# Recurrent memory attention on one core: row statistics, scaling and turning moved within a segment, and the copies of attention sums given to ScalarE

## The chip, the cores and the metric

The kernel runs on one core of a Trainium2 chip. The metric is the device time of one execution in microseconds (us); lower is better. TensorE (PE) multiplies matrices, VectorE (DVE) and ScalarE (ACT) do elementwise work, GpSimd (POOL) and SyncE (SP) mostly issue DMAs here. PEld is the loading of matmul weights. Each engine works through its own list of instructions in order and waits on semaphores for the others.

## The reference

```python
xn = layernorm(x)                                   # x: 2048 x 1024, bf16
# A: 64 segments of 32 rows, one after the other
for s in range(64):
    h = concat(mem, xn[32*s:32*s+32])               # 8 memory rows + 32 rows
    q, k, v = h @ Wq, h @ Wk, h @ Wv                # 32 heads of 128
    p = softmax(mask(q @ k.T * 128**-0.5))
    o = (p @ v) @ Wo                                # back to 1024 columns
    mem = o[:8]                                     # memory of the next segment
    out_A[s] = o[8:]
# B: a gated MLP on the 2 rows of xn with the largest xn @ w_r, added to those rows
return x + out_A + (xn + scatter(MLP(top 2 rows)))
```

Every segment needs the memory rows of the one before, so the 64 segments are a chain. Each uses all of Wq, Wk, Wv and Wo (32 MB in bf16).

## The kernel before

**Weights.** Wq, Wk, Wv and Wo are cut into 64 granules of 512 KB. 44 stay in SBUF. The other 20 are streamed again for every segment: SyncE issues their DMAs (line 368, `g<-wsc` in the trace) into five slots, and a slot is filled again when the last matmul that reads it is done. Two of the 20 are held in part or whole in PSUM and copied back (`BK<-KEPT`, `g<-KEPT`).

**Main rows and left rows.** A segment's matmuls take 32 rows: 24 main rows of the segment (`XM`) and the 8 memory rows. The 8 left rows of each segment (`XL`) do not depend on the memory for q, k and v, so those of four segments are gathered: a group G is four segments with j = 0, 1, 2, 3, and the 32 left rows of group G+1 are multiplied in passing while group G's weights are there (`PSl<-...`, `left_pass`). They are loaded in the segment with j = 0 (`get_left`, tile `BX`, a POOL DMA), normalised, turned, and are ready as `STL` at the end of that segment. Segments with j = 1, 2, 3 have no such work. Of the 16 segments with j = 0, those of groups 1 to 14 (s = 4 to 56) do it in the steady form.

**A segment in the program.** Six phases p = 0 to 5 (q and k of the first 16 heads, q and k of the second, v of both) with eight granules kc = 0 to 7 each (line 854). Then the output projection, w = 0 to 15, two heads each (`project`, lines 576 and 580). Other work is hung between matmuls by a table: `hook(p, kc, fn)` runs fn when the program reaches that place, and so fixes the order on every engine. Hooks of one place run in the order in which they were set.

- `scores(half)` multiplies q and k of 16 heads and does the mask, the maximum and its subtraction on DVE (lines 674 to 689). `exponent` is one ACT instruction (693). `soften` does sum, reciprocal, scaling and transposes on DVE (698 to 722). `attend(half, ph)` multiplies with v (739, 741) and copies the sums to SBUF (750 to `OT`, 752 to `OTL`).
- The layer norm of the next 24 rows has its steps apart. `part_stats` (198, 199) and `split_stats` (202 to 205) are DVE work on a quarter row per partition, `sum_stats` two small matmuls (209), `take_sums` an ACT copy (213), `spread_of` two DVE instructions (216, 218), `root_of` two ACT instructions (221, 222). `norm_seg` then scales on DVE (293 to 298: `XN`, and x itself in place, as the residual), `norm_left` does so for the left rows (341).
- `turn_rows` transposes `XN`, and in j = 0 the left rows, on PE (305) into the PSUM bank `BT`; `new_st` copies them on ACT to `ST` (319) and `STL` (323). In that bank also lie the second half of each block of attention sums (`OPB`) and the statistics' sums (`SUMS`).
- After w = 15, DVE adds up the result (928), PE turns it and DVE puts the memory rows into `ST` (328): the next segment's matmuls begin.

Of the kernel before, what the change touches and what calls it, by code (L numbers as in the profile page):

```python
# [51 lines left out]
def kernel(  # L52
# [16 lines left out]
    nc = tc.nc  # L69
# [8 lines left out]
    NSEG = S // SEG  # L78
    NT = S // P
# [74 lines left out]
    X = [const.tile([P, 256], BF16, name=f"X{b}") for b in range(2)]  # L154
# [13 lines left out]
    ROWS = [SW[:, 10:14], SW[:, 16:20]]  # L168
# [28 lines left out]
    def part_stats(x):  # L197
        nc.vector.bn_stats(out=S6, in_=x)
        nc.vector.bn_aggr(out=AV, in_=S6)
# [7 lines left out]
    def sum_stats(sums):  # L207
        for c in range(2):
            nc.tensor.matmul(sums, lhsT=S4, rhs=HL[:, 2 * c:2 * c + 2], start=(c == 0), stop=(c == 1),
                             skip_group_check=True)  # L210

    def take_sums(r, sums):
        nc.scalar.copy(out=r[:, 0:2], in_=sums)  # L213

    def spread_of(r):
        nc.vector.scalar_tensor_tensor(out=r[:, 2:3], in0=r[:, 0:1], scalar=r[:, 0:1], in1=r[:, 1:2],
                                       op0=ALU.mult, op1=ALU.subtract)
        nc.vector.tensor_scalar(out=r[:, 2:3], in0=r[:, 2:3], scalar1=0.0, scalar2=1e-5, op0=ALU.min, op1=ALU.subtract)

    def root_of(r):  # L220
        nc.scalar.activation(out=r[:, 3:4], in_=r[:, 2:3], func=ACTF.Ln, scale=-1.0)
        nc.scalar.activation(out=r[:, 3:4], in_=r[:, 3:4], func=ACTF.Exp, scale=-0.5)
# [66 lines left out]
    def norm_seg(s):  # L289

        x = X[s % 2]
        ab, m, r = AB, ROWS[0][:, 0:1], ROWS[0][:, 3:4]
        nc.vector.tensor_scalar(out=ab[:, 0:1], in0=r, scalar1=1.0, scalar2=KMSK, op0=ALU.add, op1=ALU.mult)
        nc.vector.tensor_scalar(out=ab[:, 1:2], in0=m, scalar1=r, scalar2=NMSK, op0=ALU.mult, op1=ALU.mult)
        xn = front.tile([P, 256], BF16, tag="st", name="XN")
        nc.vector.tensor_scalar(out=xn[:, :], in0=x[:, :], scalar1=m, scalar2=r,
                                op0=ALU.subtract, op1=ALU.mult)
        nc.vector.tensor_scalar(out=x[:, :], in0=x[:, :], scalar1=ab[:, 0:1], scalar2=ab[:, 1:2],
                                op0=ALU.mult, op1=ALU.add)
        return xn  # L300

    def turn(src, at=0):
        PTx = PTB[:, 256 * at:256 * (at + 1)].rearrange("p (c g r) -> p c g r", c=2, g=4)
        for c in range(2):
            nc.tensor.transpose(out=PTx[:, c, :, :].rearrange("p g r -> p (g r)"), in_=src[:, c * P:(c + 1) * P],
                                identity=IDENT[:, :])
        return PTx

    def gview(st):
        return st.rearrange("p (g c) r -> p c g r", c=2)  # L310

    def turn_rows(xn, xl):

        return turn(xn), turn(xl, 1) if xl is not None else None

    def new_st(turned):
        PTx, PTl = turned
        st = front.tile([P, KC, SEG], BF16, tag="st", name="ST")
        nc.scalar.copy(out=gview(st)[:, :, :, 0:XM], in_=PTx[:, :, :, 0:XM])
        if PTl is None:  # L320
            return st, None
        stl = one.tile([P, KC, SEG], BF16, tag="stl", name="STL")
        nc.scalar.copy(out=gview(stl), in_=PTl[:, :, :, :])
        return st, stl
# [15 lines left out]
    def norm_left(t):  # L340
        nc.vector.tensor_scalar(out=t[:, :], in0=t[:, :], scalar1=ROWS[1][:, 0:1], scalar2=ROWS[1][:, 3:4],
                                op0=ALU.subtract, op1=ALU.mult)
# [112 lines left out]
    xn = norm_seg(0)  # L455
# [178 lines left out]
    for s in range(NSEG):  # L634
        G, j = divmod(s, 4)
# [6 lines left out]
        QT, KT, PTs, OT, nxt, sums = {}, {}, {}, {}, {}, {}  # L642
        hooks = {}

        def hook(p, kc, fn):
            hooks.setdefault((p, kc), []).append(fn)
# [79 lines left out]
        def attend(half, ph, turn_too=None):  # L726
            if half not in sums:
                if half not in OT:
                    OT[half] = one.tile([P, 4, 4, SEG], BF16, tag=("kt", "bC")[half], name="OT")
                if half == 0:  # L730
                    nxt["wo"] = psA.tile([P, 512], F32, tag="acc", name="WO")
                sums[half] = [BS[:, 0:4 * NK] if half else nxt["wo"][:, 256:256 + 4 * NK], OPB]
            PTm, PTl = PTs[half]
            with_sums = (half, ph) == (0, 1) and s + 1 < NSEG
            for il in range(4):
                for jl in range(2):
                    q0 = 32 * (2 * ph + jl)
                    o = sums[half][jl][:, il * NK:(il + 1) * NK]
                    nc.tensor.matmul(o, lhsT=VM[half][q0:q0 + 32, il * P:(il + 1) * P], rhs=PTm[q0:q0 + 32, il, 0:NK],  # L739
                                     start=True, stop=False, tile_position=(q0, 0), skip_group_check=True)  # L740
                    nc.tensor.matmul(o, lhsT=VL[half][q0:q0 + 32, il * P:(il + 1) * P], rhs=PTl[q0:q0 + 32, il, 0:NK],
                                     start=False, stop=True, tile_position=(q0, 0), skip_group_check=True)
            if with_sums:
                sum_stats(SUMS)
            if turn_too is not None:
                turn_too()
            for jl in range(2):
                ov = sums[half][jl].rearrange("p (i q) -> p i q", i=4)
                copy = nc.scalar.copy if half == 0 or jl == 0 or ph == 1 else nc.vector.tensor_copy
                copy(out=OT[half][:, 2 * ph + jl, :, :], in_=ov[:, :, 0:SEG])  # L750
                h0 = 16 * half + 8 * ph + 4 * jl
                copy(out=left_out()[:, h0:h0 + 4, j, :], in_=ov[:, :, SEG:NK])
            if with_sums:
                take_sums(ROWS[0], SUMS)
# [57 lines left out]
        if j == 0 and G + 1 < NT:  # L812
            hook(*((4, 1) if s == 0 else (1, 0)), get_left)
            if s > 0:
                hook(2, 5, lambda: part_stats(nxt["xl"]))
                hook(2, 5, split_stats)
                hook(4, 0, lambda: sum_stats(SUMS))
                hook(4, 1, lambda: take_sums(ROWS[1], SUMS))
                hook(4, 2, lambda: spread_of(ROWS[1]))
                hook(5, 0, lambda: root_of(ROWS[1]))  # L820
            else:
                hook(5, 7, lambda: stats_now(nxt["xl"], ROWS[1]))
        hook(*((1, 0) if s > 0 else (2, 3)), clear_pl)
# [2 lines left out]
        hook(3, 4, lambda: soften(0))  # L826
        if s + 1 < NSEG:
            hook(2, 4, lambda: load_seg(s + 1))
        if j == 0 and G + 1 < NT:
            hook(5, 3 if s > 0 else 7, lambda: norm_left(nxt["xl"]))  # L830
        if s + 1 < NSEG:
            hook(4, 5, lambda: part_stats(X[(s + 1) % 2][:, :]))
        hook(4, 6, lambda: scores(1))
        hook(5, 0, exponent)
        if s + 1 < NSEG:
            hook(5, 0, split_stats)
        else:
            hook(1, 0, router_out)
            hook(1, 6, router_in)
# [49 lines left out]
        assert not hooks, hooks  # L889

        WO = nxt["wo"]
        if s + 1 < NSEG:
            root_of(ROWS[0])
            xn = norm_seg(s + 1)
            left_too = nxt["xl"] if j == 0 and G + 1 < NT else None
            turned = []

        def lhs_main(h):
            return OT[h // 16][:, (h % 16) // 4, h % 4, :]
# [2 lines left out]
        for w in range(16):  # L902
            if w == 5:
                attend(1, 0)
            if w == 8 and s + 1 < NSEG:
                attend(1, 1, lambda: turned.append(turn_rows(xn, left_too)))
                nxt["st"], stl = new_st(turned[0])
                STL = stl or STL
            elif w == 8:
                attend(1, 1)  # L910
            Gv = granule(48 + w)
            if w == N_WIDE:
                SUM = one.tile([P, 256], F32, tag="bE", name="SUM")
                add_halves(WO, X[s % 2], SUM, SUM)
                WO = psA.tile([P, 512], F32, tag="acc", name="WO")
            project(WO, w, Gv, lhs_main)
            held[48 + w] = Gv
            run_passes(6, w)
            if w == 9 and s + 1 < NSEG:
                new_lx(s + 1)  # L920
                bring_back(2, nc.scalar.copy)
            if w == 12 and s + 1 < NSEG:
                bring_back(0, nc.scalar.copy)
            if w == 2 and j == 3:
                xl_of[0] = load_left(G, one.tile([P, 256], BF16, tag="stl", name="OL")[:, :], True)
            release(6, w)
# [133 lines left out]
```

## Time and profile before

| | |
|---|---|
| median of 3 runs | 1890.1 us (1883.99 to 1893.26) |
| profiled execution | 1895.79 us, span 1894.1 us |
| mean granted TensorE clock | 0.949 |
| busy: PE, DVE, ACT, POOL | 85%, 53%, 41%, 24% of the span |
| DMA | 707.70 MB, mean 374 GB/s |

The first segment fills SBUF and copies the streamed weights; it ends at about 120 us. The last ends about 58 us before the end, where the MLP of the two rows follows. Between them lie 63 segments of some 27 us each. A row of the trace is read so: start, duration, engine, line, operation, what it writes and reads, how many, and in brackets the idle time of the engine just before and who ended it. Segments are told apart by the addition on line 928, which ends each.

### The profile page before, as it was taken

The numbers are of one execution on the slowest core, as the hardware profiler recorded it, in microseconds if no ns is written. First come the engines' busy times: TensorE is split into PE (matmuls) and PEld (weight loads), VectorE is DVE, ScalarE is ACT, GpSimd is POOL, SyncE is SP. The second block draws the span as 40 slices with busy tenths as digits, with TensorE's granted clock in tenths as the row PEclk, the third lists the DMA queues.
The fourth block names the chain that finished last, engine by engine and source line by source line (L and its number), as shares of the span: only waits on it lengthen the run. The fifth ranks groups of instructions, "written<-read, shape, count | busy, mean of one in ns | idle before, by whom it ended". The sixth has DMA issues, their size and how long they took to land.

```text
span 1894.1 us, 78902 instructions
## 1 busy us (share of the span) xinstructions
PE 1605.4 (85%) x33752; PEld 828.0 (44%) x33752; DVE 1010.8 (53%) x3368; ACT 768.8 (41%) x2409; POOL 455.2 (24%) x895
## 2 busy tenths in 40 slices
PE   4478989998988898899899888889889888989864
PEld 2134444444444444444444444444444444444433
DVE  2135566556555555655565555556555565565550
ACT  1034444444443444444444344444444444444330
POOL 2212313231231323123131322323132222312220
PEclk9579999999999999999999999999999999999995
DMA  9999999999999999999999999999999999999998
GB/s 368 404 366 377 365 374 381 370 385 366 380 362 376 342 373 383 372 383 355 387 370 378 363 378 377 359 381 376 388 362 376 379 377 382 365 384 373 366 402 341
DMA packets 228063, 707.70 MB, mean 374 GB/s; under 512 B 38912, under 2 KB 52832, under 8 KB 227712
## 3 DMA queue, kind: packets, MB, share of 16 engines
q1 hardware_dynamic: 190272, 666.72, 92.6%
q0 software_dynamic: 28640, 28.03, 4.6%
q10 hardware_dynamic: 8800, 7.92, 1.2%
q8 instruction: 264, 4.33, 0.9%
q14 instruction: 87, 0.71, 0.1%
HBM read 689.86 MB, written 22.29 MB: 376 GB/s over the span
## 4 chain that ended last, share of the span: by engine, by line
DMA 59%; PE 30%; DVE 6%; ACT 2%; issue 2%; POOL 1%; SPq 0%; DVEq 0%; ACTq 0%; POOLq 0%
DMA g<-wsc 46%; PE PSm L854 16%; PE PSl L567 4%; DMA BX<-in_A_x_dram 3%; PE WO L580 2%; PE BT L651 2%; DMA wres<-in_A_Wk_dram 1%; PE WO L576 1%; DMA g<-in_A_Wo_dram 1%; DMA g<-in_A_Wv_dram 1%; DMA wres<-in_A_Wv_dram 1%; DMA MW<-in_B_w_gate_dram 1%; PE WL L600 1%; DMA MW<-in_B_w_up_dram 1%; DMA X<-in_A_x_dram 1%
## 5 line engine op out<-in xcount | busy, mean ns | idle before, releaser
L854 PE MATMUL PSm<-wres,ST 128*32 128x512 bf16 x8448 | 702.5, 383 | 25.0 <-DMA wres<-in_A_Wv_dram 14.3
L854 PEld LDWEIGHTS <-ST 128*32 128x32 bf16 x12288 | 324.8, 96 | 392.3 <-issue 167.9
L854 PE MATMUL PSm<-g,ST 128*32 128x512 bf16 x3588 | 363.7, 388 | 84.2 <-DMA g<-wsc 70.0
L873 ACT CAST XB<-PSm 128x512 bf16<-128x512 f32 x256 | 150.3, 587 | 281.6 <-PE PSm L854 270.9
L483 POOL DMA_DIRECT2D LX<-ql_d x63 | 35.5, 564 | 655.5 <-PE WO L580 377.1
L567 PE MATMUL PSl<-wres,STL 128*32 128x512 bf16 x2112 | 184.5, 390 | 0.2 <-ACT XBl L878 0.2
L666 DVE COPY KT<-BT 128x512 bf16<-128x512 bf16 x112 | 45.8, 409 | 255.1 <-PE BT L651 252.4
L930 POOL DMA_DIRECT2D out_dram<-X x256 | 129.4, 512 | 210.7 <-DVE X L928 204.8
L286 POOL DMA_DIRECT2D X<-in_A_x_dram x252 | 127.4, 511 | 193.9 <-PE PSm L854 92.4
L391 ACT COPY BK<-KEPT 128x512 bf16<-128x512 bf16 x189 | 109.2, 614 | 107.3 <-PE WO L580 48.0
L580 PEld LDWEIGHTS <-OT 128*32 128x32 bf16 x4096 | 106.8, 98 | 84.5 <-issue 64.4
L576 PE MATMUL WO<-wres,OT 128*32 128x512 bf16 x1536 | 135.1, 420 | 0.0
L659 ACT COPY QT<-BT 128x512 bf16<-128x512 bf16 x128 | 74.9, 586 | 123.3 <-PE BT L490 74.4
L580 PE MATMUL WO<-g,OT 128*32 128x256 bf16 x1536 | 79.3, 283 | 49.7 <-DMA g<-wsc 43.2
L739 PEld LDWEIGHTS <-VM 32*128 32x128 bf16 x2048 | 67.3, 92 | 118.3 <-issue 84.0
L651 PE MATMUL BT<-IDENT,XB 128*128 128x128 bf16 x1024 | 101.7, 222 | 16.1 <-ACT SW L213 14.1
L651 PEld LDWEIGHTS <-XB 128*128 128x128 bf16 x1024 | 59.1, 98 | 124.3 <-ACT XB L873 74.7
L580 PE MATMUL WO<-wres,OT 128*32 128x256 bf16 x2560 | 108.5, 280 | 0.0
L883 ACT CAST VM<-PSm 128x512 bf16<-128x512 f32 x128 | 76.6, 599 | 73.7 <-PE PSm L854 73.4
L567 PEld LDWEIGHTS <-STL 128*32 128x32 bf16 x3072 | 84.6, 97 | 47.7 <-issue 4.9
L576 PEld LDWEIGHTS <-OT 128*32 128x32 bf16 x2048 | 58.5, 100 | 81.9 <-issue 55.0
L683 DVE TENSOR_TENSOR BS<-BS,CT 128x96 f32<-128x96 f32 (+1 forms) x256 | 59.0, 230 | 64.3 <-PE BS L676 59.3
(189 smaller groups left out, 2801.3 us busy)
## 6 DMA issues: line engine op xcount, KB each, us to landing
g<-wsc SPq DMA_DIRECT2D x1134, 512.0 KB, 6.1
g<-wsc SPq DMA_DIRECT2D x63, 256.0 KB, 5.8
LX<-ql_d POOLq DMA_DIRECT2D x63, 128.0 KB, 5.9
ql_d<-XBl ACTq DMA_DIRECT2D x60, 128.0 KB, 5.9
MW<-in_B_w_gate_dram SPq DMA_DIRECT2D x16, 448.0 KB, 9.0
MW<-in_B_w_up_dram SPq DMA_DIRECT2D x16, 448.0 KB, 9.1
wres<-in_A_Wk_dram SPq DMA_DIRECT2D x12, 512.0 KB, 15.3
wres<-in_A_Wq_dram SPq DMA_DIRECT2D x11, 512.0 KB, 5.2
```

The costliest lines, as they stand in the source:

```text
L286: by.dma_start(out=X[s % 2][32 * g:32 * g + XM, :], in_=x2[s * SEG:s * SEG + XM, 256 * block(g):256 * (block(g) + 1)])
L391: copy(out=back[c][:, :], in_=KEPT_COLS[KEPT_WHOLE][c])
L567: nc.tensor.matmul(PSl[32 * jq:32 * jq + 32, :], lhsT=STL[:, g % KC, :], rhs=part(Gv, jq), start=first_, stop=last_, tile_position=(0, 32 ...
L576: nc.tensor.matmul(PS[r0:r0 + 32, :], lhsT=lhs(h), rhs=Gv[:, D * hs + 512 * c:D * hs + 512 * (c + 1)], start=(w == 0), stop=(w == N_WIDE - ...
L580: nc.tensor.matmul(PS[32 * g:32 * g + 32, 0:256], lhsT=lhs(h), rhs=Gv[:, D * hs + 256 * block(g):D * hs + 256 * (block(g) + 1)], start=(w ...
L651: nc.tensor.transpose(out=PTq[:, il, :, :].rearrange("p j r -> p (j r)"), in_=XB[:, il * P:(il + 1) * P], identity=IDENT[:, :])
L659: nc.scalar.copy(out=QT[half][:, :, :], in_=pv)
L739: nc.tensor.matmul(o, lhsT=VM[half][q0:q0 + 32, il * P:(il + 1) * P], rhs=PTm[q0:q0 + 32, il, 0:NK], start=True, stop=False, tile_position ...
L854: nc.tensor.matmul(PSm[32 * jq:32 * jq + 32, :], lhsT=ST[:, 2 * block(kc // 2) + kc % 2, :], rhs=part(Gv, jq), start=(kc == 0), stop=(kc = ...
L873: nc.scalar.copy(out=XB[:, :], in_=PSm[:, :])
L883: nc.scalar.copy(out=VM[half][:, :], in_=PSm[:, :])
L930: nc.gpsimd.dma_start(out=out2[s * SEG:s * SEG + XM, 256 * block(g):256 * (block(g) + 1)], in_=OB[32 * g:32 * g + XM, :])
```

## The change

Four things change.

1. In j = 0, the statistics of the left rows on DVE are hung behind the first scores, at (2, 7) for (2, 5). Their spread goes to (5, 7) and their root and scaling behind the first block of the second half's attention, at w = 5.
2. In j = 0, the statistics of the next 24 rows go behind the second scores, to (5, 0) for (4, 5); their root and scaling go to w = 5 too. In the other segments they stay where they were, ahead of the projection.
3. The turning of the next rows was inside the last attention block at w = 8, between its matmuls and its copies. It is now by itself, at w = 11 in j = 0 and at w = 10 in the others, with the copies to `ST` and `STL` behind it.
4. All copies of attention sums are ACT's. DVE did those of one pair per segment (64 of line 750, 64 of line 752).

The order on POOL and SP is unchanged.

VectorE in a segment with j = 0, from the copy of the keys to the end of the first scores' work (`BX` holds the left rows, `BS` the scores, `SW` the statistics). Before:

```order
L666 COPY KT<-BT 128x16x32
L198 BN_STATS SW<-BX 128x6
L199 BN_AGGR SW<-SW 128x2
L202 SCALAR_TENSOR_TENSOR SW<-SW 128x1
L204 TENSOR_SCALAR SW<-SW 128x2
L205 SCALAR_TENSOR_TENSOR SW<-SW 128x2
L683 TENSOR_TENSOR BS<-BS,CT 128x4x24
L685 TENSOR_SCALAR BS<-BS,SW 128x4x8
L683 TENSOR_TENSOR BS<-BS,CT 128x4x8
L688 TENSOR_REDUCE NM<-BS 128x8
L689 TENSOR_TENSOR BS<-BS,NM 128x320
```

The same place now:

```order
L666 COPY KT<-BT 128x16x32
L683 TENSOR_TENSOR BS<-BS,CT 128x4x24
L685 TENSOR_SCALAR BS<-BS,SW 128x4x8
L683 TENSOR_TENSOR BS<-BS,CT 128x4x8
L688 TENSOR_REDUCE NM<-BS 128x8
L689 TENSOR_TENSOR BS<-BS,NM 128x320
L198 BN_STATS SW<-BX 128x6
L199 BN_AGGR SW<-SW 128x2
L202 SCALAR_TENSOR_TENSOR SW<-SW 128x1
L204 TENSOR_SCALAR SW<-SW 128x2
L205 SCALAR_TENSOR_TENSOR SW<-SW 128x2
```

The five instructions on the left rows, the first of which needs their DMA, stand behind the scores.

ScalarE in the same segment, from the copy of v to the copies of the turned rows (`BS` and `BT` hold the attention sums of one pair). Before:

```order
L883 CAST VM<-PSm 128x512
L221 ACTIVATE SW<-SW 128x1
L222 ACTIVATE SW<-SW 128x1
L750 CAST OT<-BS 128x128
L752 CAST OTL<-BS 128x4x8
L750 CAST OT<-BS 128x128
L752 CAST OTL<-BS 128x4x8
L750 CAST OT<-BT 128x128
L752 CAST OTL<-BT 128x4x8
L319 COPY ST<-BT 128x2x4x24
L323 COPY STL<-BT 128x2x4x32
```

The same place now, from the first block's second pair on:

```order
L750 CAST OT<-BT 128x128
L752 CAST OTL<-BT 128x4x8
L221 ACTIVATE SW<-SW 128x1
L222 ACTIVATE SW<-SW 128x1
L221 ACTIVATE SW<-SW 128x1
L222 ACTIVATE SW<-SW 128x1
L750 CAST OT<-BS 128x128
L752 CAST OTL<-BS 128x4x8
L750 CAST OT<-BT 128x128
L752 CAST OTL<-BT 128x4x8
L391 COPY BK<-KEPT_190 128x512
L319 COPY ST<-BT 128x2x4x24
```

Both roots now stand between the two blocks' copies, the pair from `BT` is ACT's in both blocks, and the copy to `ST` has come behind a weight copy.

TensorE at the turning of the rows in j = 0, with what each instruction waits for. Before, right behind the last attention matmul:

```order
L741 MATMUL BT<-PT_3819,VL 128x40
L305 LDWEIGHTS XN
L305 MATMUL BT<-IDENT,XN 128x128
L305 LDWEIGHTS XN
L305 MATMUL BT<-IDENT,XN 128x128
L305 LDWEIGHTS BX [waits DMASW5_49,DMASW6_49,DMASW4_49,DMASW3_49]
L305 MATMUL BT<-IDENT,BX 128x128
```

Now, behind the matmuls of w = 10:

```order
L580 MATMUL WO<-wres_1012,OT 32x256
L305 LDWEIGHTS XN [waits DVE_49]
L305 MATMUL BT<-IDENT,XN 128x128 [waits Activation_49]
L305 LDWEIGHTS XN
L305 MATMUL BT<-IDENT,XN 128x128
L305 LDWEIGHTS BX [waits DMASW5_49,DMASW4_49,DMASW6_49,DMASW3_49,DVE_49]
L305 MATMUL BT<-IDENT,BX 128x128
```

The turning has moved three steps of the projection on, and has two waits of its own: for the scaling on DVE and for copies on ACT.

The diff:

```diff
@@ attend
-                copy = nc.scalar.copy if half == 0 or jl == 0 or ph == 1 else nc.vector.tensor_copy
+                copy = nc.scalar.copy
@@ hooks
         if j == 0 and G + 1 < NT:
             hook(*((4, 1) if s == 0 else (1, 0)), get_left)
             if s > 0:
-                hook(2, 5, lambda: part_stats(nxt["xl"]))
-                hook(2, 5, split_stats)
+                hook(2, 7, lambda: part_stats(nxt["xl"]))
+                hook(2, 7, split_stats)
                 hook(4, 0, lambda: sum_stats(SUMS))
                 hook(4, 1, lambda: take_sums(ROWS[1], SUMS))
-                hook(4, 2, lambda: spread_of(ROWS[1]))
-                hook(5, 0, lambda: root_of(ROWS[1]))
+                hook(5, 7, lambda: spread_of(ROWS[1]))
...
-        if j == 0 and G + 1 < NT:
-            hook(5, 3 if s > 0 else 7, lambda: norm_left(nxt["xl"]))
-        if s + 1 < NSEG:
-            hook(4, 5, lambda: part_stats(X[(s + 1) % 2][:, :]))
         hook(4, 6, lambda: scores(1))
         hook(5, 0, exponent)
         if s + 1 < NSEG:
+            hook(*((5, 0) if j == 0 else (4, 5)), lambda: part_stats(X[(s + 1) % 2][:, :]))
             hook(5, 0, split_stats)
@@ projection
-        if s + 1 < NSEG:
+        left_too = nxt["xl"] if j == 0 and G + 1 < NT else None
+        later = left_too is not None
+        def norm_next():
+            nxt["xn"] = norm_seg(s + 1)
+            if later:
+                norm_left(left_too)
+        if s + 1 < NSEG and not later:
             root_of(ROWS[0])
-            xn = norm_seg(s + 1)
-            left_too = nxt["xl"] if j == 0 and G + 1 < NT else None
-            turned = []
+            norm_next()
...
             if w == 5:
                 attend(1, 0)
-            if w == 8 and s + 1 < NSEG:
-                attend(1, 1, lambda: turned.append(turn_rows(xn, left_too)))
-                nxt["st"], stl = new_st(turned[0])
+                if later:
+                    root_of(ROWS[0])
+                    if s > 0:
+                        root_of(ROWS[1])
+                    norm_next()
+            if w == 8:
+                attend(1, 1)
+            if w == (11 if later else 10) and s + 1 < NSEG:
+                nxt["st"], stl = new_st(turn_rows(nxt["xn"], left_too))
                 STL = stl or STL
-            elif w == 8:
-                attend(1, 1)
```

## The prediction

> **What bounds the kernel now.** I read the page first.
>
> ```profile
> PE 1605.4 (85%) x33752; PEld 828.0 (44%) x33752; DVE 1010.8 (53%) x3368; ACT 768.8 (41%) x2409; POOL 455.2 (24%) x895
> DMA packets 228063, 707.70 MB, mean 374 GB/s; under 512 B 38912, under 2 KB 52832, under 8 KB 227712
> ```
>
> PE is at 85%, and the DMAs move 374 GB/s. The waits of PE show which of the two leads, and where another engine does.
>
> ```profile
> PE PSm L854 <- DMA g<-wsc: 70.0, 147, 1.9
> PE WO L580 <- DMA g<-wsc: 43.2, 77, 1.4
> PE WO L739 <- ACT OTL L752: 15.1, 14, 1.6
> PE BT L651 <- ACT SW L213: 14.1, 14, 2.0
> PE BT L739 <- DVE OTL L752: 3.6, 13, 0.8
> ```
>
> PE waits mostly for weights, for 70 and 43 us. Two waits for ACT stand out since each has 14 cases: they are the segments with j = 0 and left rows, one per group, with 15.1 + 14.1 = 29.2 us, or 2.1 us each. Then I cut the span into segments, here some of those with j = 0 of groups 1 to 14 (from, to, length, busy times, granted clock, DMA share, GB/s).
>
> ```profile
> core 0: us, PE busy (x) PEld busy (x) DVE busy (x) ACT busy (x) POOL busy (x), PEclk, DMA share, GB/s
> 417.11:446.56 29.45, 25.57 (x508) 13.04 (x503) 18.22 (x65) 13.22 (x44) 10.26 (x19) 0.88 0.98 362
> ...
> 856.90:886.38 29.48, 26.00 (x508) 13.25 (x504) 18.21 (x66) 13.32 (x44) 10.34 (x19) 0.88 0.99 364
> 965.88:993.98 28.10, 24.46 (x506) 12.44 (x502) 18.22 (x66) 13.28 (x44) 10.34 (x19) 0.94 0.99 370
> 1074.17:1105.11 30.94, 26.04 (x505) 12.84 (x501) 18.25 (x65) 13.29 (x44) 10.34 (x19) 0.89 0.96 341
> ...
> sum 397.12, PE 345.16 PEld 174.07 DVE 255.04 ACT 185.53 POOL 144.45; mean PE 24.65 PEld 12.43 DVE 18.22 ACT 13.25 POOL 10.32
> ```
>
> The same sums for the 14 segments each with j = 1 and j = 3:
>
> ```profile
> sum 379.10, PE 336.10 PEld 177.37 DVE 207.06 ACT 154.20 POOL 69.01; mean PE 24.01 PEld 12.67 DVE 14.79 ACT 11.01 POOL 4.93
> sum 374.20, PE 347.83 PEld 179.95 DVE 203.47 ACT 165.89 POOL 101.55; mean PE 24.85 PEld 12.85 DVE 14.53 ACT 11.85 POOL 7.25
> ```
>
> A segment with j = 0 takes 28.37 us (397.12 / 14), one with j = 1 27.08: 1.29 us more, 18.0 us in all. Of the 14, 12 show a clock of 0.94 or less. The chain that ended last says through what j = 0 runs, in the segment from 965.88:
>
> ```profile
> 969.69 1.66 POOL BX L337 x3
> 971.36 5.65 DMA BX<-in_A_x_dram
> 977.12 0.44 DVE SW L198
> ...
> 985.85 0.42 ACT BS L693
> ```
>
> From the load of the left rows it goes through DVE to the second exponent, then to PE. In the other segments it alternates between weights and PE. So time can be had in 14 of 63 segments, and the path there is DVE's.
>
> **The change part by part.** DVE in that segment (start, duration, instruction):
>
> ```profile
> 977.12 0.43 DVE L198 BATCH_NORM_STATS2 SW<-BX 128x6 f32<-128x256 bf16 x1 [1.17 <-DMA BX<-in_A_x_dram]
> ...
> 978.34 0.26 DVE L683 TENSOR_TENSOR BS<-BS,CT 128x96 f32<-128x96 f32 x1
> ...
> 980.10 0.84 DVE L621 TENSOR_TENSOR LF<-WL,LF 64x256 f32<-64x256 f32 x2
> 980.97 0.49 DVE L698 TENSOR_REDUCE DN<-BS 128x8 f32<-128x320 f32 x1
> ...
> 983.05 0.18 DVE L216 SCALAR_TENSOR_TENSOR SW<-SW 128x1 f32<-128x1 f32 x1
> ...
> 983.99 0.24 DVE L683 TENSOR_TENSOR BS<-BS,CT 128x96 f32<-128x96 f32 x1
> ...
> 988.38 0.31 DVE L341 TENSOR_SCALAR BX<-BX,SW 128x256 bf16<-128x256 bf16 x1
> ...
> 989.51 0.21 DVE L293 TENSOR_SCALAR SW<-SW 128x1 f32<-128x1 f32 x1 [0.50 <-ACT SW L222]
> ```
>
> And PE, at the last matmul of the first scores, the two waits, and the last two attention blocks:
>
> ```profile
> 976.45 0.18 PE L676 MATMUL BS<-KT,QKL 128*8 128x40 bf16 x1
> 981.37 0.38 PE L651 MATMUL BT<-IDENT,XB 128*128 128x128 bf16 x4 [0.99 <-ACT SW L213]
> 986.60 0.17 PE L739 MATMUL WO<-PT,VM 32*128 32x40 bf16 x1 [1.36 <-ACT OTL L752]
> 989.12 0.21 PE L739 MATMUL BS<-PT,VM 32*128 32x40 bf16 x1
> 990.90 0.21 PE L739 MATMUL BS<-PT,VM 32*128 32x40 bf16 x1
> 992.49 0.39 PE L580 MATMUL WO<-g,OT 128*32 128x256 bf16 x8
> ```
>
> *Left statistics behind the first scores.* The scores are in PSUM at 976.65, but DVE stands at the left rows until 977.12 and handles them until 978.34. Now it starts the scores at about 976.7; the rows land meanwhile. The statistics still come before the first softmax, so their 1.22 us stay on the path; the wait of 0.47 us goes. Its bounds: nothing where the rows were there before the scores, 1.17 us (the whole idle time in the bracket) at most here.
>
> *Spread and next rows' statistics behind the second scores.* 983.05 to 983.99, 0.94 us, stood on the path ahead of the second scores. They now run behind them, partly under the exponent (0.42 us). The second exponent thus starts at 976.7 + 1.85 (scores, 978.34 to 980.19) + 1.22 + 0.87 (the sum at 980.10) + 2.08 (softmax, 980.97 to 983.05) + 1.86 (scores, 983.99 to 985.85) = 984.58, for 985.85: 1.27 us earlier. The matmuls at 986.60 wait for the copies behind that exponent, so PE comes there by 985.35. At 981.37 most of the 0.99 us goes too, since ACT is no longer held by the first exponent; some 0.3 us appear where PE needs the late left statistics, and some 0.5 where the second scores need the first softmax's reads done. DVE still leads, so these don't add to the 1.27.
>
> *Scaling at w = 5.* The second softmax starts after 1.2 us of the moved statistics and takes 2.1: it ends at 987.9, and PE does the first block at 988.0 for 989.12. From here a new chain runs: four ACT copies, four roots, five DVE instructions. ACT starts its copies 0.5 us after PE's block, two pairs take 0.7, the roots 0.9 (rows below), L293 to L298 took 1.0 from 989.51, L341 takes 0.3: 3.4 us, cut to some 3.1 as L341 alone needs the second root. Scaled at 991.1 to 991.4.
>
> ```profile
> L222 ACT ACTIVATE SW<-SW 128x1 f32<-128x1 f32 x96 | 19.5, 203 | 3.0
> L750 ACT CAST OT<-BT 128x128 bf16<-128x128 f32 x192 | 54.6, 284 | 1.0 <-PE BT L305 1.0
> L750 DVE CAST OT<-BT 128x128 bf16<-128x128 f32 x64 | 18.3, 286 | 6.2 <-PE BT L741 6.0
> ```
>
> *Turning at w = 11.* PE would be there at about 990.4 at full clock, so it waits up to 1 us, turns in 0.44 us and goes on at 991.6, where it was at 992.49: 0.9 us is left of the 1.27. Ahead of that wait w = 8 runs over 1 us earlier than at 991.82, and its slot is refilled earlier; queued behind the wait are w = 11 to 15, and the addition on DVE, which now follows the scaling and ends at about 993.1, before PE is done.
>
> *Turning at w = 10 elsewhere.* The turning wrote to the bank that ACT is to read, between matmuls and copies; now it waits until ACT has copied. ACT needs 0.5 + 0.7 us from the block's start, PE 0.36 + 0.44 (w = 8 and 9): up to 0.4 us of new wait. Between 0 and 0.4 us in 49 segments I take zero, because PE waits for weights right behind: 43.2 us in 77 waits of line 580. Without that cover it costs up to 19 us. For it, the turning's 0.22 us (two matmuls) no longer delay the slot read at w = 8. I give that 2 us in all; bounds 0 and 0.22 x 63 = 14.
>
> *ACT for DVE.* 64 x (0.286 + 0.181) = 30 us leave DVE; ACT's price is equal (284 for 286 ns). ACT is idle 59% of the span, and the pair is copied before the roots instead of behind the scaling, which ends the 3.6 us of waits for DVE. In j = 0 its 0.35 us are in the 3.1 above. Otherwise nothing.
>
> **The sum.** PE gains 0.9 us in each of 14 segments: 12.6. The stream bounds this: with j = 0 it holds two more sets of four DMAs, the load and the store of left rows.
>
> ```profile
> out_dram<-OL POOLq DMA_DIRECT2D x64, 16.0 KB, 5.3
> BX<-in_A_x_dram POOLq DMA_DIRECT2D x56, 16.0 KB, 5.0
> ```
>
> These 128 KB are 0.35 us at 374 GB/s, so at the rate of j = 1 a segment would still be 0.94 us faster: 13.2. But the longest, 30.94 us, has a DMA share of 0.96 and 341 GB/s, which no wait here explains; I leave out its excess over the others, 3 us. That makes some 9.6, and 2 for the slots: 11.5 us. The profiled execution would take 1884; it was 0.3% above the median. From the median: **1879 us**, 0.6% faster.
>
> **The clock.** Around the stall of that segment:
>
> ```profile
> 985.00:988.40 3.40, 1.98 (x46) 1.12 (x42) 3.19 (x12) 2.12 (x11) 0.00 (x0) 1.00 0.95 356
> 988.40:991.80 3.40, 3.40 (x60) 1.30 (x48) 2.21 (x11) 1.12 (x6) 0.00 (x0) 0.51 0.99 377
> ```
>
> A stretch with PE 58% busy is followed by one at half clock. If less stall cures this, the segments at 0.88 gain most: 29.45 and 29.48 exceed 27.08 + 0.35 by 2.0 us each. If not, the 11 segments without those three (27.93 us on average) still hold 0.5 us each: 5.5 us, giving 1885.
>
> [...]
>
> **Rivals.** *The stream takes it back* (1884 to 1890): five slots refill when PE frees them, but with the DMA share at 0.99 PE may only wait for weights instead. For: 113 us of such waits. Against: j = 1 moves more per us (its 27.08). 0.30. *The clock falls as before* (1885): for it, that the half clock follows 58% and not an idle stretch, and so may follow a smaller loss too; against it, that the stall right before it is the one that shortens. 0.10. *The new wait leads* (slower): at w = 10 in 49 segments, 0.4 us each uncovered is 19.6 - 11.5 = 8 us more than before, 1898. It decides from 0.25 us exposed. For: the added wait on ACT at a place with little slack. Against: the 77 waits for weights behind it. 0.08. *The change does not do what it says*: the left rows land so late that the statistics still hold the softmax; they were there 0.47 us after the scores, and the scores take 1.85. Within the range.
>
> **How the numbers follow.** Forecast (1871 to 1880.6): 0.52. Stream: 0.30. Clock: 0.10. New wait: 0.08, half of it within 0.5%. What can be told from no change is about 0.5%, or 9.5 us. Faster 0.52, same 0.42, slower 0.06. The range goes from 1867 (14 us for the slots added in part) to 1892, where the second case ends and the third begins.
>
> **What would show it.** In the profile after: the waits of L651 for L213 and L739 for L752 fall from 29 us to under 12; the second exponent in j = 0 starts about 8 us after the first scores, for 9.2; PE waits at the turning, under 1 us with j = 0 and under 0.4 elsewhere, with fewer waits for weights behind; the sum over j = 0 falls from 397 to about 386, the others stay; the chain no longer passes through the left rows' load. I am wrong if j = 0 shortens and j = 1 grows by as much, or if the clock falls as before.

## The result and the profile after

The changed kernel takes 1876.7 us (median of 7 runs, 1872.1 to 1881.9), the kernel before 1891.2 us (7 runs, 1884.0 to 1893.7). The ratio is 0.993 with a 95% interval of 0.9909 to 0.9951: 0.7% faster, against 0.6% forecast. The profiled execution took 1876.71 us at a mean granted clock of 0.962 (0.949 before).

The page of the changed kernel: busy times, DMA, and the shares of the chain that ended last.

```profile
PE 1596.5 (85%) x33752; PEld 816.9 (44%) x33752; DVE 991.5 (53%) x3240; ACT 782.6 (42%) x2537; POOL 455.0 (24%) x895
DMA packets 228063, 707.70 MB, mean 377 GB/s; under 512 B 38912, under 2 KB 52832, under 8 KB 227712
...
DMA 64%; PE 32%; DVE 2%; issue 1%; ACT 1%; SPq 0%; POOL 0%; DVEq 0%; ACTq 0%
```

128 instructions went from DVE to ACT. The bytes are the same, and they moved at 377 instead of 374 GB/s. DVE's share of the last chain, 6% before, is 2%.

What PE waited for in the changed kernel (total us, times, longest):

```profile
PE PSm L850 <- DMA g<-wsc: 74.2, 154, 1.7
PE WO L580 <- DMA g<-wsc: 42.6, 83, 1.6
PE WO L576 <- DMA g<-wsc: 28.4, 61, 1.4
...
PE BT L209 <- DVE SW L204: 17.3, 17, 10.4
...
PE WO L739 <- ACT OTL L752: 2.9, 7, 0.6
...
PE BS L674 <- DVE BX L717: 2.6, 14, 0.2
```

Two rows of the kernel before that belong beside these:

```profile
PE WO L576 <- DMA g<-wsc: 20.0, 43, 1.5
PE BT L209 <- DVE SW L204: 14.9, 3, 10.3
```

The wait of L651 for L213 (14.1 us) is gone, and that of L739 fell from 15.1 to 2.9 us. Something small came in their place: 14 waits of 0.17 us at the statistics' matmul (209: 17.3 us less the 14.9 that stood there before), and 14 of 0.2 us at the second scores (674). More came as waits for weights: line 850 (854 before) had 70.0 us and now 74.2, and line 576, the steps of the projection before w = 8, had 20.0 and now 28.4. Nearly all of it came in the 14 segments with j = 0 and left rows: summed over these alone, from the idle times in the two traces, PE's waits for weights went from 16.8 to 36.2 us, and its waits for anything else from 32.9 to 8.2.

The 14 segments with j = 0 and left rows, some of them and their sum (from, to, length, busy times with counts, clock, DMA share, GB/s):

```profile
200.54:228.84 28.30, 25.44 (x508) 12.41 (x504) 17.86 (x63) 13.37 (x46) 10.33 (x19) 0.88 1.00 371
309.09:335.27 26.18, 23.74 (x506) 11.86 (x501) 17.95 (x63) 13.27 (x46) 10.33 (x19) 1.00 1.02 388
...
524.62:551.55 26.93, 24.73 (x508) 12.20 (x504) 17.94 (x63) 13.32 (x47) 10.26 (x19) 0.94 1.00 377
...
1062.11:1089.63 27.52, 23.89 (x505) 12.24 (x501) 17.96 (x63) 13.50 (x46) 10.37 (x19) 1.00 1.01 379
...
sum 384.01, PE 335.35 PEld 168.89 DVE 250.87 ACT 186.88 POOL 144.32; mean PE 23.95 PEld 12.06 DVE 17.92 ACT 13.35 POOL 10.31
```

The sums for j = 1 and j = 3 in the changed kernel:

```profile
sum 373.45, PE 336.66 PEld 175.76 DVE 202.76 ACT 158.88 POOL 68.99; mean PE 24.05 PEld 12.55 DVE 14.48 ACT 11.35 POOL 4.93
sum 375.61, PE 347.18 PEld 177.47 DVE 199.99 ACT 171.15 POOL 101.41; mean PE 24.80 PEld 12.68 DVE 14.28 ACT 12.23 POOL 7.24
```

In this execution j = 0 fell by 13.1 us (397.12 to 384.01), j = 1 by 5.7, and j = 3 rose by 1.4. Twelve of the 14 stand at a clock of 1.00, where two did before. Such sums come from one execution, and the experiments show that they scatter by several us; the place of the gain is therefore taken from timed runs below.

The order on DVE and ACT in the segment from 1062.11 (start, duration, instruction):

```profile
1072.89 0.27 DVE L683 TENSOR_TENSOR BS<-BS,CT 128x96 f32<-128x96 f32 x1 [0.77 <-PE BS L676]
...
1074.65 0.42 DVE L198 BATCH_NORM_STATS2 SW<-BX 128x6 f32<-128x256 bf16 x1
...
1080.60 0.42 DVE L198 BATCH_NORM_STATS2 SW<-X 128x6 f32<-128x256 bf16 x1
1080.73 0.42 ACT L693 ACTIVATE BS<-BS 128x320 f32<-128x320 f32 x1 [1.16 <-DVE BS L689]
...
1085.76 0.21 DVE L293 TENSOR_SCALAR SW<-SW 128x1 f32<-128x1 f32 x1 [1.20 <-ACT SW L222]
...
1086.71 0.34 DVE L341 TENSOR_SCALAR BX<-BX,SW 128x256 bf16<-128x256 bf16 x1
```

PE in the same segment, from the last matmul of the first scores to the turning:

```profile
1072.63 0.18 PE L676 MATMUL BS<-KT,QKL 128*8 128x40 bf16 x1
...
1075.80 0.36 PE L209 MATMUL BT<-SW,S 128*128 128x2 bf16 x2 [0.16 <-DVE SW L204]
...
1081.47 0.17 PE L739 MATMUL WO<-PT,VM 32*128 32x40 bf16 x1 [0.62 <-ACT OTL L752]
...
1083.58 0.40 PE L576 MATMUL WO<-g,OT 128*32 128x512 bf16 x4 [0.47 <-DMA g<-wsc]
...
1085.17 0.40 PE L576 MATMUL WO<-g,OT 128*32 128x512 bf16 x4 [0.46 <-DMA g<-wsc]
...
1086.48 0.40 PE L580 MATMUL WO<-g,OT 128*32 128x256 bf16 x8 [0.17 <-DMA g<-wsc]
...
1087.25 0.29 PE L305 MATMUL BT<-IDENT,XN 128*128 128x128 bf16 x2
```

The first scores end on PE at 1072.81, and DVE takes them 0.08 us later. The second exponent starts 7.92 us behind them (9.22 in the segment read before the change), and the rows are scaled at 1087.05, 14.2 us behind them. PE stands 0.62 us for the copies behind that exponent, where it stood 1.36. It now waits for weights ahead of w = 8 (0.47 and 0.46 us, at w = 2 and w = 5) and reaches the turning 0.2 us after the scaling is done. The chain of this segment says the same:

```profile
1076.53 5.71 DMA g<-wsc
...
1082.72 6.20 DMA g<-wsc
...
1088.97 0.62 PE WO L580 x16
```

Up to the statistics' matmul it still passes DVE's first scores and the statistics of the left rows, though no longer their load. From that matmul on, it goes through two refills of a weight slot and no longer through DVE.

### The profile page after: what moved, and what is told of

The parts are those of the page before. It is cut to its first block, busy times and chain, and to the rows that moved or that the text cites. A ratio compares the mean times of both kernels' runs of the same rounds, so it can differ in the third digit from the quotient of the medians.

```text
span 1875.1 us, 78929 instructions
## 1 busy us (share of the span) xinstructions
PE 1596.5 (85%) x33752; PEld 816.9 (44%) x33752; DVE 991.5 (53%) x3240; ACT 782.6 (42%) x2537; POOL 455.0 (24%) x895
## 3 DMA queue, kind: packets, MB, share of 16 engines
q10 hardware_dynamic: 8800, 7.92, 1.2%
## 4 chain that ended last, share of the span: by engine, by line
DMA 64%; PE 32%; DVE 2%; issue 1%; ACT 1%; SPq 0%; POOL 0%; DVEq 0%; ACTq 0%
DMA g<-wsc 55%; PE PSm L850 17%; PE PSl L567 4%; PE WO L580 2%; PE BT L651 2%; DMA wres<-in_A_Wk_dram 1%; PE WL L600 1%; DMA g<-in_A_Wo_dram 1%; DMA g<-in_A_Wv_dram 1%; DMA wres<-in_A_Wv_dram 1%; PE WO L576 1%; DMA MW<-in_B_w_gate_dram 1%; DMA MW<-in_B_w_up_dram 1%; DMA g<-in_A_Wq_dram 1%; DMA g<-in_B_w_down_dram 1%
## 5 line engine op out<-in xcount | busy, mean ns | idle before, releaser
L850 PE MATMUL PSm<-g,ST 128*32 128x512 bf16 x3588 | 361.8, 385 | 88.3 <-DMA g<-wsc 74.2
L580 PEld LDWEIGHTS <-OT 128*32 128x32 bf16 x4096 | 101.1, 97 | 92.3 <-issue 62.9
L576 PE MATMUL WO<-wres,OT 128*32 128x512 bf16 x1536 | 126.6, 393 | 0.2 <-issue 0.2
L580 PE MATMUL WO<-wres,OT 128*32 128x256 bf16 x2560 | 116.5, 278 | 0.0
L739 PEld LDWEIGHTS <-VM 32*128 32x128 bf16 x2048 | 64.3, 91 | 112.7 <-issue 90.6
L651 PEld LDWEIGHTS <-XB 128*128 128x128 bf16 x1024 | 59.1, 98 | 109.8 <-ACT XB L869 64.1
L651 PE MATMUL BT<-IDENT,XB 128*128 128x128 bf16 x1024 | 101.9, 222 | 2.2 <-ACT QKL L502 1.5
L576 PEld LDWEIGHTS <-OT 128*32 128x32 bf16 x2048 | 57.7, 96 | 87.4 <-issue 59.0
```

Of the source, the lines that this page charges most:

```text
L576: nc.tensor.matmul(PS[r0:r0 + 32, :], lhsT=lhs(h), rhs=Gv[:, D * hs + 512 * c:D * hs + 512 * (c + 1)], start=(w == 0), stop=(w == N_WIDE - ...
L580: nc.tensor.matmul(PS[32 * g:32 * g + 32, 0:256], lhsT=lhs(h), rhs=Gv[:, D * hs + 256 * block(g):D * hs + 256 * (block(g) + 1)], start=(w ...
L651: nc.tensor.transpose(out=PTq[:, il, :, :].rearrange("p j r -> p (j r)"), in_=XB[:, il * P:(il + 1) * P], identity=IDENT[:, :])
L850: nc.tensor.matmul(PSm[32 * jq:32 * jq + 32, :], lhsT=ST[:, 2 * block(kc // 2) + kc % 2, :], rhs=part(Gv, jq), start=(kc == 0), stop=(kc = ...
```

## The experiments

The kernels were timed in three series. Each ratio sets a kernel's runs against runs of the kernel before from the same series (medians 1889.3, 1891.2 and 1891.7 us), with a 95% interval in brackets. It is not the quotient of two medians, so that 1884.9 us can go with 0.9991.

### Where the gain is: the change in j = 0 alone, and everywhere else alone

`j0_only` keeps, in segments without left rows, DVE's copy of the pair and the turning inside the last block:

```diff
-                copy = nc.scalar.copy
+                copy = nc.scalar.copy if half == 0 or jl == 0 or ph == 1 or (j == 0 and G + 1 < NT) else nc.vector.tensor_copy
...
+            if w == 8 and s + 1 < NSEG and not later:
+                attend(1, 1, lambda: turned.append(turn_rows(nxt["xn"], left_too)))
...
-            if w == (11 if later else 10) and s + 1 < NSEG:
+            if w == 11 and later:
```

> All of the change in the segments with j = 0 and left rows, none of it in the others (their turning stays inside the last attention block at w = 8, one pair of sums stays with DVE). Theory A, the shorter DVE path in j = 0 is the gain and j = 1 gains because j = 0 hands over earlier: 12 to 16 us faster than before, the sum over j = 0 near 384 us, j = 1 near 374. Rival B, the other segments' new order gives the 6 us of j = 1: 8 to 11 us faster, j = 1 stays near 379.

`others_only` is the kernel before with these two parts of the change in the segments without left rows and nothing in j = 0.

> The counterpart: the turning at w = 10 and ACT's copies only in segments without left rows. Theory A: within 3 us of before, j = 0 near 397 us. Rival B: 4 to 7 us faster, in j = 1. Rival C, the turning's new wait for ACT costs something that j = 0 hid: 2 to 8 us slower.

Measured: `j0_only` 1875.4 us, 0.9934 [0.9909, 0.996]; `others_only` 1889.3 us, 1.001 [0.9985, 1.0036]. So the gain lies in the segments with j = 0 and left rows. In the others the added wait for ACT and the freed slots together cost or bring nothing that can be told: by the interval they gain at most 0.15%, 3 us, and cost at most 0.36%, 7 us.

### Whether it is the clock

`before_filler` is the kernel before with 20 more matmuls into an unread PSUM tile, in j = 0 right ahead of the wait for the copies behind the second exponent. It adds work and takes nothing away:

```diff
+        if j == 0 and s > 0 and G + 1 < NT:
+            hook(5, 6, lambda: filler(5))
```

> The kernel before, with 20 matmuls (5 of each column group, some 1.1 us at full clock) that nobody reads, set ahead of the last block of the first half's attention in j = 0 with left rows, where PE waited 1.08 us on average. They add work but no result. Theory K, most of the loss in j = 0 is the clock that falls after the stall: the granted clock stays at 1.00 in at least 10 of 14 segments, and the time is 5 to 9 us shorter than before although PE has more to do. Rival S, the stall itself is the loss: within 2 us of before or slower, at whatever clock.

Measured: 1887.3 us, 1.0002 [0.9981, 1.0023]. Some of its segments with j = 0, and their sum:

```profile
199.60:227.61 28.01, 24.29 (x527) 12.66 (x522) 18.22 (x66) 13.26 (x44) 10.36 (x19) 1.00 0.99 362
311.54:340.49 28.95, 24.85 (x526) 12.67 (x522) 18.22 (x66) 13.25 (x44) 10.28 (x19) 1.00 1.00 368
420.67:449.33 28.66, 25.03 (x527) 12.78 (x523) 18.35 (x66) 13.28 (x44) 10.29 (x19) 1.00 0.99 361
...
sum 393.45, PE 343.83 PEld 177.65 DVE 254.89 ACT 184.94 POOL 144.84; mean PE 24.56 PEld 12.69 DVE 18.21 ACT 13.21 POOL 10.35
```

The clock is 1.00 in 13 of the 14, and the time is the same. Curing the clock in this way brings at most 0.19%, 3.6 us, with the filler's own cost in it. That cost can be estimated: the 20 matmuls take some 1.25 us in the trace, in a stall of 1.08 us on average, which is some 2 us more in 14 segments. What the clock is worth when the stall is gone too was not run. The waits of PE in this kernel show where it stood instead:

```profile
PE BT L651 <- ACT SW L213: 16.2, 14, 1.7
...
PE BT L739 <- DVE OTL L752: 10.1, 23, 0.8
...
PE WO L739 <- ACT OTL L752: 1.9, 6, 0.5
```

The filled stall is gone from the third row, but PE came to the last attention block before DVE had copied the pair of the block ahead: 3.6 us of that wait became 10.1 (in the 14 segments alone 0.8 became 7.0).

### The parts one by one

`left_stats_only` is the kernel before with only the left rows' statistics moved:

```diff
-                hook(2, 5, lambda: part_stats(nxt["xl"]))
-                hook(2, 5, split_stats)
+                hook(2, 7, lambda: part_stats(nxt["xl"]))
+                hook(2, 7, split_stats)
```

> The kernel before with only the left rows' statistics behind the first scores, from (2, 5) to (2, 7). By the prediction's path the second exponent comes 0.5 us earlier (the wait for the rows' landing), of 1.27 in all: 3 to 6 us faster than before, with the wait of line 739 for ACT at 0.6 us on average for 1.08. Rival: the 0.94 us of spread and next statistics still in front of the second scores keep the stall and the clock's fall: within 2 us of before.

Measured: 1884.9 us, 0.9991 [0.9971, 1.0011]. That is the rival's forecast. The wait at L651 is gone, but the one ahead of the projection stands, at 1.2 us on average for the 0.6 expected:

```profile
PE WO L739 <- ACT OTL L752: 17.1, 14, 1.6
```

`after_stats_back` is the changed kernel with this part alone undone (2, 7 back to 2, 5).

> The changed kernel with the left rows' statistics ahead of the first scores again, at (2, 5); all else changed. Path theory: DVE waits for the rows' landing again (0.5 us as in the segment of the prediction, up to 1.1 on average by the idle time before line 198), so the second exponent comes 0.5 to 1 us later than in the changed kernel and 3 to 8 us of its 13 are lost: 5 to 10 us faster than before. Rival, the order of the left statistics is worth nothing, as it was by itself: 11 to 15 us faster.

Measured: 1881.6 us, 0.9942 [0.9906, 0.9977], and L651 waits for L213 as before. Both ways this part comes out near 0.1%, and neither tells it from nothing.

`turn_only` is the kernel before with only the turning moved, to w = 11 and w = 10:

```diff
-            if w == 8 and s + 1 < NSEG:
-                attend(1, 1, lambda: turned.append(turn_rows(xn, left_too)))
...
+            if w == (11 if left_too is not None else 10) and s + 1 < NSEG:
+                nxt["st"], stl = new_st(turn_rows(xn, left_too))
```

> The kernel before with only the turning moved: out of the last attention block, to w = 11 in j = 0 with left rows and w = 10 elsewhere. Turning theory (formed from the traces so far: the scaled rows are there some 15 us after the first scores in the kernel before and in the changed one alike, and with the turning at w = 8 the weight slot read at w = 8 stood behind them): the first read at w = 8 comes 0.5 us or more earlier in j = 0, and 5 to 9 us of the 13 are had by this alone. Path theory of the prediction (the second exponent 1.27 us earlier is the gain): within 3 us of before.

Measured: 1887.2 us, 0.9968 [0.995, 0.9986]: about half of the gain, with the waits for ACT and DVE still there. But the mark that was named for it did not come: the first read at w = 8 stands at 15.45 us, for 15.55 before (table below). That moving the turning gains is shown; how it gains is not.

```profile
PE BT L651 <- ACT SW L213: 19.8, 14, 2.0
...
PE WO L739 <- ACT OTL L752: 17.0, 15, 1.6
...
PE BT L739 <- DVE OTL L752: 8.5, 22, 0.8
```

`act_only` is the kernel before with `copy = nc.scalar.copy` and nothing else.

> The kernel before with only ACT's copies of the last pair. Both theories: within 3 us of before, since the turning still holds w = 8. Rival, the wait of the last attention block for DVE's copies, which stand behind the scaling, is what holds it: 4 to 8 us faster.

Measured: 1888.0 us, 0.9977 [0.9958, 0.9995], that is 1 to 8 us, which does not separate the two forecasts. The wait of L739 for DVE is gone, and the two for ACT remain:

```profile
PE WO L739 <- ACT OTL L752: 14.0, 15, 1.4
PE BT L651 <- ACT SW L213: 12.1, 14, 1.5
```

The wait that went can't be what was gained in j = 0: of its 13 cases in the kernel before, 12 stand in segments without left rows, where `others_only` finds nothing.

### How much a later second exponent costs

`after_delay` and `after_delay4` are the changed kernel with two and four more unused rounds of the left rows' statistics on DVE ahead of the second scores, in j = 0:

```diff
+        if j == 0 and s > 0 and G + 1 < NT:
+            for _ in range(2):
+                hook(4, 5, lambda: part_stats(nxt["xl"]))
```

> The changed kernel with four more DVE instructions ahead of the second scores in j = 0 with left rows (the statistics of the left rows twice again, not used): 2 x 0.61 = 1.2 us more on the path that was shortened by 1.3. Path theory: nearly all of the gain is gone, 0 to 4 us faster than before, j = 0 near 395 us in sum. Rival, the weight stream takes a delay of 1 us without loss and something else made the gain: 9 to 14 us faster.

> The same with eight instructions, 2.5 us. Path theory: straight on, 14 x 1.2 = 17 us more than with four: 10 to 18 us slower than before. Rival, the stream takes part of it: within 5 us of before.

Measured: two rounds put the exponent 1.2 us later (8.09 to 9.31 us behind the first scores, mean of 14), and the time is 1881.3 us, 0.9942 [0.9922, 0.9962]. Four put it at 10.66 us, and the time is 1898.9 us, 1.0045 [1.0024, 1.0067]. The first dose costs 0.1%, some 2 us in 14 segments, which can't be told from nothing; the second, some 19 us. Against the kernel before, four rounds are 8.5 us slower, between the two forecasts. Waits of PE with two rounds:

```profile
PE WO L576 <- DMA g<-wsc: 18.9, 42, 1.7
PE WO L739 <- ACT OTL L752: 17.0, 16, 1.8
```

and with four:

```profile
PE WO L739 <- ACT OTL L752: 38.7, 14, 3.2
```

With the first dose 14 us of waiting for ACT came back, but 9.5 us of waits for weights at line 576 (28.4 to 18.9) went; in the 14 segments, over all lines, 36.2 us of them became 18.4. That is the cover: in the changed kernel the refill of the slots allows PE to be about a microsecond later. Behind it the delay counts about in full: 1.35 us x 14 = 18.9. The clock may have a part in that: it is 1.00 in 8 of the 14 segments with two rounds, and in none with four.

### Where the turning should stand

The changed kernel with the turning at another w; `after_turn_8` (w = 8 in j = 0, in front of the weights), `after_turn_12` (12 everywhere) and `after_turn_13` (13 everywhere):

```diff
-            if w == (11 if later else 10) and s + 1 < NSEG:
+            if w == 12 and s + 1 < NSEG:
```

> The changed kernel with the turning back at w = 8 in j = 0 with left rows, behind the last attention block; statistics and scaling stay as changed, the other segments too. Turning theory: the wait for the scaled rows stands ahead of w = 8 again, whose first read goes from 14.2 to over 15 us after the first scores, and most of the gain is lost: within 5 us of before. Path theory: 9 to 13 us faster than before, since the second exponent is as early as in the changed kernel.

> The changed kernel with the turning at w = 12 in all segments, for 10 and 11. PE's new wait at the turning (9.9 us in all in the changed kernel's trace, 46 cases in segments without left rows) should go. If it was uncovered: 15 to 22 us faster than before, thus 4 to 8 better than the changed kernel. If weights covered it: the same as the changed kernel, 11 to 15 us faster than before. If the later copies to ST and STL hold the next segment: less.

> The changed kernel with the turning at w = 13 in all segments, one further than the version with 12, which was 0.990 of before. If the turning goes on to gain by standing behind more weight reads: 0.985 to 0.990. If 12 and 11 differ by chance and the wait is covered: 0.990 to 0.994. If the copies to ST now come too late for the memory rows: PE waits for line 319 or 323 at the next turning, 0.994 or more.

Measured: 1885.4 us, 0.9961 [0.9942, 0.998] at 8; 1872.4 us, 0.9896 [0.9868, 0.9924] at 12; 1886.4 us, 0.9981 [0.9957, 1.0004] at 13. The kernel with 8 is 7.4 us faster than before, between the two forecasts: a little under half of the gain is lost. There PE waits for the copies of the bank that it turns into (waits of `after_turn_8`):

```profile
PE BT L305 <- ACT OTL L752: 9.2, 13, 0.8
```

The kernel before had no such wait, since it turned ahead of the copies. So this run does not undo the move alone, and its loss may be that wait's.

At 12, the wait at the turning that was to go only became smaller. In the changed kernel and in `after_turn_12`:

```profile
PEld L305 <- DVE SUM L590: 9.9, 46, 0.4
PEld L305 <- DVE SUM L590: 7.9, 30, 0.4
```

At 13, the next transposes find the copies to `ST` not done (waits of `after_turn_13`):

```profile
PE BT L305 <- ACT ST L319: 12.4, 10, 2.6
```

So the place has a window: too early it holds the weights behind it, too late the segment's end. Twelve has the lowest time of all kernels run, but its interval overlaps that of the change, so whether it is better stays open.

### The kernels side by side

Mean over the 14 segments, us from the start of the last matmul of the first scores, worked out from the starts of instructions in one profiled execution each: the second exponent (693), the first matmul at w = 8, which reads a streamed slot, and the next segment's first read of the granule that refills that slot.

| kernel | ratio | exponent | read at w = 8 | next read of the slot |
|---|---|---|---|---|
| before | 1 | 9.49 | 15.55 | 22.59 |
| before_filler | 1.0002 | 9.64 | 15.37 | 22.53 |
| left_stats_only | 0.9991 | 9.12 | 15.05 | 22.09 |
| act_only | 0.9977 | 9.38 | 15.11 | 22.21 |
| turn_only | 0.9968 | 9.91 | 15.45 | 22.56 |
| after_delay | 0.9942 | 9.31 | 14.57 | 21.89 |
| after | 0.993 | 8.09 | 14.22 | 21.76 |
| after_delay4 | 1.0045 | 10.66 | 16.39 | 23.49 |
| after_stats_back | 0.9942 | 8.80 | 14.51 | 22.09 |
| after_turn_8 | 0.9961 | 8.11 | 15.44 | 22.30 |
| after_turn_12 | 0.9896 | 8.09 | 14.45 | 22.01 |
| after_turn_13 | 0.9981 | 8.12 | 14.26 | 22.13 |

`after_delay` and the kernel before have nearly the same exponent (9.31 and 9.49), but the read at w = 8 comes a microsecond earlier, and the time is 0.6% lower. `after_turn_8` is the counterpart: it has the exponent of the changed kernel and the read of the kernel before, and is 0.4% faster where the changed kernel is 0.7%. The closest pair is `left_stats_only` and `after_delay`. Their exponents (9.12 and 9.31) and their waits of L739 for ACT (17.1 and 17.0 us) are nearly alike, neither waits at L651 for L213 any more, and the clock is 1.00 in 6 and 8 of 14 segments; yet their intervals lie apart, by 0.5% at the middle. What they differ in is the turning, ACT's copies, the scaling at w = 5, and the left rows' spread and the next rows' statistics. So most of the gain is not the exponent's; it is had by these other parts.

Counted from the exponent, the read at w = 8 comes 6.06 us later before, 5.73 in `act_only`, 5.54 in `turn_only` and 5.26 in `after_delay`. That fits two parts that each shorten this piece, but 5.73 in `before_filler`, where the clock is 1.00 in 13 of the 14 segments for 2 before, suggests that the clock shortens it too. From before to after the next read of the slot comes 0.83 us earlier, 11.6 us in 14 segments, near the 14.5 us between the medians. That is not proof: in `left_stats_only` it comes 0.50 us earlier, 7 us in 14 segments, with 0.1% gained. The table is one execution each and does not rank all kernels: `turn_only` gains without an earlier read, and `after_turn_13` has the early read without the gain.

The j = 0 sums of single executions rank them even less: 386.3 us for `left_stats_only` (0.9991), 391.4 for `after_turn_12` (0.9896), 381.4 for `after_turn_13` (0.9981).

## Why the prediction was right, and where it was not

*The time and its place.* Right: 1879 forecast, 1876.7 measured, in j = 0, by `j0_only` and `others_only`. The j = 0 sum was forecast at 386 and came to 384, in one execution of a sum that scatters by more than that. The place was read from the rows. That the time came so near is in good part luck, since the sum reached it through a term that failed.

*Left rows' statistics; spread and next statistics.* The marks moved as worked out. DVE's wait for the rows went, the exponent came 1.40 us earlier on the mean (forecast 1.27), and the waits at L651 and L739 fell from 29.2 to 2.9 us (under 12 forecast). The new waits are 0.17 us each at line 209 (17.3 less 14.9, by 14; 0.3 forecast) and 0.2 us at line 674 (0.5 forecast).

*The conversion of the exponent's 1.27 us into time.* This step failed. It gave PE 0.9 us in each of 14 segments, 12.6 us before the deduction, for the earlier exponent, and nothing for ACT's copies. Putting 1.2 us of it back cost some 2 us (0.9942 for 0.993; with both intervals, added in squares, at most 8), not 12. The parts that the prediction costed at little or nothing measured more by themselves: the turning 0.32%, or 6 us, and ACT's copies 0.23%, or 4 us; the left rows' statistics 0.09%. Together that is 0.64%, near the whole 0.7%, but each has an interval of about 0.2% to either side, so the division among them is only rough. Moving the scaling to w = 5 was not run by itself, nor were the left rows' spread and the next rows' statistics.

For the turning a row had been there. In j = 0 it was four matmuls, 0.44 us, between the last attention matmul and the weights at w = 8; 14 x 0.44 = 6.2 us is as much as `turn_only` gained. The agreement proves little, since that read came only 0.10 us earlier in its trace. The prediction saw the release of the slot, but only as 2 us, for two matmuls in all 63 segments; by `others_only` at most 3 us are to be had in 49 of them. For ACT's copies, the wait of L739 for DVE's copies was 3.6 us, and the prediction said that it ends without adding it to the sum. But 12 of its 13 cases lie in the other segments, so that row does not explain a gain in j = 0. Why these parts gain stays open.

*The stream.* As a rival for the whole it is out, but it is the answer for the exponent's part: PE arrives earlier at the projection and waits there for weights (line 576, 20.0 to 28.4 us; in the 14 segments 1.6 to 11.0). The prediction had named fewer waits for weights as a sign; in j = 0 they more than doubled, from 16.8 to 36.2 us.

*The clock.* The prediction let 6 of its 11.5 us hang on the clock (1885 against 1879). The clock did recover, to 1.00 in 12 of 14 for 2 before, but in the kernel before a cured clock brought at most 3.6 us, with the filler's cost of some 2 us in it. The rival, that the clock falls as before, did not come.

*Scaling at w = 5, turning at w = 11.* The rows were scaled at 14.2 us in the segment shown. At the turning PE waited for the scaled left rows 1.8 us in 8 cases, under the 1 us each that was allowed: it comes later itself, held by weights. *Turning at w = 10 elsewhere.* No cost that can be told, as forecast: the new wait is there, 9.9 us in 46 cases, 0.2 us each for the 0 to 0.4 expected (the view puts it down to DVE's addition at line 590, the prediction to ACT's copies), but `others_only` is at 1.001. The rival of 19.6 us uncovered is out.

## What to carry to other kernels

A wait's length tells how long an engine stood, not what its removal brings: with a stream behind it, ask which instruction releases the next slot and what stands in front of that one, and run each such part by itself. Here a four-matmul transpose and a pair of copies, costed at little or nothing, gained some 0.3% and 0.2%. Put some of the removed delay back in two doses; a flat first dose and a steep second one show how much slack the next limit leaves. Time the change in one class of segments alone before its gain is read out of the sums of a single trace.

## What the runs showed of the hardware

The granted clock fell behind stretches in which PE was partly busy: before the change, in the segment of the prediction, a clock of 0.51 (988.40 to 991.80) followed a stretch of 3.40 us in which PE was busy for 1.98 and stood for 1.36 at most at a time. In the 12 segments with j = 0 where it fell, PE was busy for 45 to 70% of a stretch of that length right ahead of the fall. With twenty further matmuls in that stall, some 1.25 us, it was 1.00 in 13 of 14 segments, for 2 before, and with stalls of up to 3.2 us (`after_delay4`) all 14 were at 0.94 or less. A lower clock and lost time also came apart: in the kernel before, a clock cured by 20 added matmuls changed the time by 0.02% [-0.19%, 0.23%].
